# A linear-attention and GELU block: kv in 128-row blocks, 1/den by Ln and Exp, other places for the GpSimd adds of z

## The chip, the cores and the metric

One core of one Trainium2 chip. The metric is the device time of one execution in microseconds (us). TensorE does the matmuls, VectorE, ScalarE and GpSimd the elementwise work. In profile lines PE is TensorE, PEld its weight loads, DVE VectorE, ACT ScalarE, POOL GpSimd; L206 is line 206 of that kernel's file. Most executions of a kernel lie within 0.5 us, with a tail about 1 to 2 us higher; the trace comes from one execution.

## The reference, cut to what matters

```python
# x: (1, 2048, 640) bf16; H = 32 heads of 20 columns; F = 1536
xn  = layernorm(x)
q, k, v = split(xn @ wqkv)
pq, pk  = phi(q), phi(k)             # phi(t) = (t+1 if t > 0 else exp(t)) + 1e-6
kv  = einsum("bhsd,bhse->bhde", pk, v)
z   = einsum("bhsd->bhd", pk)        # sum of pk over the 2048 tokens
num = einsum("bhqd,bhde->bhqe", pq, kv)
den = einsum("bhqd,bhd->bhq", pq, z)[..., None] + 1e-6
out = x + (num / den) @ wo + gelu(xn @ w1 + b1) @ w2 + b2
```

## The kernel before

The 2048 tokens are 16 tiles of 128, in four groups of four. For each group g, TensorE makes K (tokens by columns), then Q (columns by tokens), then, for groups 0 to 2, twelve blocks of h = x1·w1, whose GELU ScalarE computes. While TensorE does h, VectorE makes the statistics, the reciprocal standard deviations (by Newton steps on 128x4 numbers) and the norms of the *next* group; TensorE transposes those tiles between the last h blocks. phi costs ScalarE an Exp and VectorE two operations for each 512 columns. The sum z of pk over tokens is gathered by GpSimd, one 128x640 add for each tile.

```python
def emit_norm(t, c0=0, c1=NC):                       # VectorE, bf16 in and out
    nc.vector.tensor_scalar(out=xn[:, t, ds], in0=x_all[:, t, ds],
        scalar1=mv[:, t, 0:1], scalar2=rstd[:, t : t + 1], op0=subtract, op1=mult)

def phi(dst, ps, shaped):
    nc.scalar.activation(out=e[:], in_=ps[:], func=ACT.Exp)
    nc.vector.tensor_scalar(out=e[:], in0=e[:], scalar1=1.0, scalar2=1e-6, op0=min, op1=add)
    nc.vector.scalar_tensor_tensor(out=dst, in0=shaped(ps), scalar=0.0, in1=shaped(e), op0=max, op1=add)

def emit_Kphi(t):
    ...
        if g > 0: emit_zacc(g)                       # adds of z behind the phi of K

def emit_zacc(g):                                    # 4 adds for a group, 3 for group 0
    for u in range(max(1, g * TPG), (g + 1) * TPG):
        nc.gpsimd.tensor_tensor(out=zsum if u == NT - 1 else zacc[:],
            in0=pk[:, 0, :] if u == 1 else zacc[:], in1=pk[:, u, :], op=ALU.add)

for g in range(NG):
    ...                                              # K and Q of group g
    for j in range(NJ if g < NG - 1 else 0):         # NJ = 12, TPG = 4
        emit_h(g, j)
        if g == 0 and j == NJ - 1:                   # hold GpSimd back to the last GELU
            nc.gpsimd.tensor_copy(out=Z3t[:, 0, 0:1], in_=hT[0][:, j, 0:1])
            emit_zacc(0)
            emit_masks()
        if j < TPG: emit_stats(t1 + j)
        if j == TPG: emit_rstd_vector(t1, t1 + TPG)  # Newton
        if TPG <= j < 2 * TPG: emit_norm(t1 + j - TPG)
        if j > 2 * TPG: emit_T(t1 + j - 2 * TPG - 1, nc.scalar.copy)
        if j == NJ - 1: emit_T(t1 + TPG - 1, nc.scalar.copy)
```

After the groups come G = xnᵀ·pk, den and its quotient (a VectorE reciprocal), then kv = wvᵀ·G for each window of heads and KVW = kv·wo, and last the output, in which `hT·w2` and `pqT·KVW` are added up in one bank.

```python
nc.vector.reciprocal(out=recT[:], in_=den[:])
...
for c in range(NC):                                  # kv: 25 matmuls of 140 columns
    for j in range(NC):
        nc.tensor.matmul(ps[:, 0:n], lhsT=wv[:, j, c*P:(c+1)*P], rhs=GT[:, j, h0*DH : h1*DH], ...)
    nc.vector.tensor_tensor(... gmask ...)
for m in range(NC):                                  # KVW: 26 matmuls of 320 columns, as the
    ...                                              # windows overlap the 128-row blocks
        for ic, c in enumerate(cs):
            nc.tensor.matmul(ps[:, 0:HALF], lhsT=kvT[:, c, m*P:(m+1)*P], rhs=wo[:, c, ns], ...)
```

## Time and profile before

| | before |
|---|---|
| median of 6 runs (range) | 217.94 us (217.52 to 218.53) |
| span of the profiled run, TensorE clock | 215.8 us, 1.0 |
| TensorE busy | 208.4 us |
| TensorE waits before the transposes of groups 1 and 2 | 1.42 and 0.31 us |
| kv, KVW (from their first matmul to the next matmul of h) | 1.57 and 3.53 us |

The busy line of the page of before, and the line of the chain of work that ended last, by engine. In the first, busy us, share of the span and instructions.

```profile
PE 208.4 (97%) x1373; PEld 120.8 (56%) x1390; DVE 108.2 (50%) x251; ACT 82.4 (38%) x132; POOL 55.3 (26%) x60
...
PE 74%; DVE 17%; ACT 3%; DMA 2%; issue 2%; SPq 0%; DVEq 0%
```

TensorE is at 97%, so the kernel gains only by fewer streamed columns or by fewer TensorE waits. The chain credits VectorE with 17%, but only because it follows VectorE's queue back from a wait; most of that time TensorE was busy as well. So read the waits themselves: below, TensorE's waits in before, with the releaser, us in total, number and longest.

```profile
PE mm L215 <- DVE xn L206: 2.0, 3, 1.4
PE mm L159 <- DVE hT_80 L128: 1.3, 1, 1.3
PE mm L236 <- ACT xnT L216: 0.5, 1, 0.5
```

L215 is the transpose, L206 the norm. Two of its three waits are in the loop. Now the timeline of before around the transposes of group 0 (start, us, engine, line, operation, in the last column the tensor written and those read, the count, and in brackets the idle time ahead of it).

```profile
29.07 1.51 DVE L206 TENSOR_SCALAR xn<-x_all,mv,rstd 128x640 bf16<-128x640 bf16 x4
...
29.72 0.44 PE L215 MATMUL mm<-identity,xn 128*128 128x128 bf16 x5
...
33.53 1.39 POOL L270 TENSOR_TENSOR zacc<-pk 128x640 f32<-128x640 bf16 x1
```

In group 0 the four norms run in 1.51 us, end at 30.58, and the transposes begin at 29.72 without a wait. GpSimd's adds come 3 us later. The same view of before, around group 1:

```profile
47.96 5.83 POOL L270 TENSOR_TENSOR zacc<-zacc,pk 128x640 f32<-128x640 f32 x4
...
52.37 0.17 DVE L188 TENSOR_SCALAR newton<-newton 128x4 int32<-128x4 int32 x1
52.57 1.25 DVE L192 TENSOR_SCALAR rstd<-newton 128x4 int32<-128x4 int32 x1
...
55.70 1.51 DVE L206 TENSOR_SCALAR xn<-x_all,mv,rstd 128x640 bf16<-128x640 bf16 x4
...
56.20 0.45 PE L215 MATMUL mm<-identity,xn 128*128 128x128 bf16 x5 [1.42 <-DVE xn L206]
```

Here GpSimd's four adds (5.83 us, so 1.46 each) lie beside VectorE's Newton steps. One of these takes 1.25 us where its neighbour takes 0.17: it stands until an add is over, at 53.8. The norms come late, and TensorE waits 1.42 us at 56.20. The last view of before is the timeline of the later stages:

```profile
105.91 3.36 DVE L402 RECIPROCAL recT<-mm 128x512 bf16<-128x512 f32 x1 [5.18 <-PE mm L397]
...
110.25 0.40 PE L409 MATMUL mm<-recT,Em_96 32*128 32x512 bf16 x4
...
124.46 1.73 PE L435 MATMUL mm<-GT,wv 128*128 128x140 bf16 x25
...
126.03 3.40 PE L288 MATMUL mm<-xnT,w_88 128*128 128x512 bf16 x14
...
129.26 3.69 PE L453 MATMUL mm<-wo,late 128*128 128x320 bf16 x26
...
132.79 1.24 PE L288 MATMUL mm<-xnT,w_88 128*128 128x512 bf16 x5
```

The reciprocal, on VectorE, ends at 109.27; its reader (L409) stands in TensorE's order behind other work and starts at 110.25 without a wait. kv runs from 124.46 to 126.03 and KVW from 129.26 to 132.79.

### The profile page before, as it was taken

How to read it: one execution, taken by the hardware profiler on the slowest of the kernel's cores; microseconds unless marked ns; L12 is line 12 of the kernel's file. 1: busy time of each engine (PE TensorE's matmuls, PEld its weight loads, DVE VectorE, ACT ScalarE, POOL GpSimd, SP SyncE). 2: the span in 40 equal slices, each digit the busy share in tenths (PEclk: the TensorE clock that was granted, in tenths of full speed). 3: DMA queues.
4: the chain of work that ended last, by engine and by line, in shares of the span. 5: the costliest groups of instructions: out<-in, count | busy, mean ns of one | idle time of the engine just before them, and what ended most of it. 6: DMA issues, size and time to landing. Idle time of an engine off the chain costs nothing.

```text
span 215.8 us, 3378 instructions
## 1 busy us (share of the span) xinstructions
PE 208.4 (97%) x1373; PEld 120.8 (56%) x1390; DVE 108.2 (50%) x251; ACT 82.4 (38%) x132; POOL 55.3 (26%) x60
## 2 busy tenths in 40 slices
PE   7899999999799999999999999999999999999994
PEld 2454455444454445545554565477777777777763
DVE  3878952999539992695374425812212212212211
ACT  3576779586686868751112746500000000000000
POOL 1000007899004600069999800000000000000000
PEclk9999999999999999999999999999999999999999
DMA  6999950000000000000000000000000010010011
GB/s 204 381 354 351 363 205 3 2 0 0 0 3 0 0 0 3 0 2 2 3 0 0 3 0 0 3 27 34 33 30 30 30 63 31 30 33 30 30 64 30
DMA packets 9727, 12.83 MB, mean 59 GB/s; under 512 B 2160, under 2 KB 8560, under 8 KB 9712
## 3 DMA queue, kind: packets, MB, share of 16 engines
q1 hardware_dynamic: 9712, 12.62, 17.1%
q8 instruction: 11, 0.18, 0.3%
q14 instruction: 4, 0.03, 0.1%
HBM read 10.00 MB, written 2.62 MB: 58 GB/s over the span
## 4 chain that ended last, share of the span: by engine, by line
PE 74%; DVE 17%; ACT 3%; DMA 2%; issue 2%; SPq 0%; DVEq 0%
PE mm L471 24%; PE mm L288 14%; PE mm L475 10%; PE mm L361 8%; PE mm L279 5%; PE mm L236 4%; DVE e L221 4%; DVE pk L224 3%; DVE pqT L224 3%; DVE stats L170 3%; PE mm L370 2%; DMA x_all<-in_A_x_dram 2%; PE mm L215 2%; PE mm L453 2%; ACT xnT L216 1%
## 5 line engine op out<-in xcount | busy, mean ns | idle before, releaser
L288 PE MATMUL mm<-xnT,w_88 128*128 128x512 bf16 x232 | 53.7, 379 | 0.4
L479 DVE TENSOR_TENSOR late<-mm,x_all 128x320 bf16<-128x320 f32 (+2 forms) x32 | 15.7, 491 | 58.5 <-PE mm L475 58.5
L288 PEld LDWEIGHTS <-w_88 128*128 128x128 bf16 x240 | 23.0, 98 | 26.2 <-issue 0.5
L220 ACT ACTIVATE e<-mm 128x512 bf16<-128x512 f32 x40 | 23.1, 597 | 12.9 <-PE mm L279 3.4
L221 DVE TENSOR_SCALAR e<-e 128x512 bf16<-128x512 bf16 x40 | 17.9, 448 | 19.2 <-ACT e L220 19.2
L270 POOL TENSOR_TENSOR zacc<-zacc,pk 128x640 f32<-128x640 f32 x13 | 18.3, 1408 | 34.5 <-DVE pk L224 33.6
L475 PE MATMUL mm<-late,pqT 128*128 128x320 bf16 (+2 forms) x160 | 27.0, 299 | 0.0
L279 PE MATMUL mm<-xnT,wqk 128*128 128x512 bf16 x98 | 22.0, 379 | 0.1
L353 POOL TENSOR_TENSOR x_all<-x_all,b2b 128x640 bf16<-128x640 bf16 x16 | 21.8, 1400 | 0.0
L236 PE MATMUL mm<-wqk,xnT 128*128 128x512 bf16 x77 | 19.9, 379 | 0.7 <-ACT xnT L216 0.5
L475 PEld LDWEIGHTS <-pqT 128*128 128x128 bf16 x160 | 15.5, 98 | 6.3
L361 PE MATMUL mm<-pk,xn 128*128 128x512 bf16 x77 | 17.8, 379 | 0.3 <-issue 0.2
L279 PEld LDWEIGHTS <-wqk 128*128 128x128 bf16 x100 | 9.6, 98 | 10.8
L414 DVE TENSOR_TENSOR pqT<-pqT,mm 128x512 bf16<-128x512 bf16 x20 | 12.3, 681 | 6.0 <-PE mm L409 6.0
L170 DVE BATCH_NORM_STATS2 stats<-x_all 128x6 f32<-128x320 bf16 x32 | 13.8, 467 | 2.7 <-DMA x_all<-in_A_x_dram 2.7
L471 PE MATMUL mm<-w_90,hT_82 128*128 128x320 bf16 x96 | 14.3, 299 | 0.0
L471 PE MATMUL mm<-w_90,hT_80 128*128 128x320 bf16 x96 | 14.3, 299 | 0.0
L471 PE MATMUL mm<-w_90,hT_81 128*128 128x320 bf16 x96 | 14.3, 299 | 0.0
L471 PE MATMUL mm<-w_90,hT_1148 128*128 128x320 bf16 (+2 forms) x95 | 14.3, 298 | 0.1
L224 DVE SCALAR_TENSOR_TENSOR pk<-mm,e 128x512 bf16<-128x512 f32 x20 | 13.8, 692 | 1.0
L224 DVE SCALAR_TENSOR_TENSOR pqT<-mm,e 128x512 bf16<-128x512 f32 x20 | 13.8, 692 | 0.7
L361 PEld LDWEIGHTS <-xn 128*128 128x128 bf16 x80 | 7.5, 98 | 9.1 <-issue 0.7
(70 smaller groups left out, 201.2 us busy)
## 6 DMA issues: line engine op xcount, KB each, us to landing
out_dram<-late SPq DMA_DIRECT2D x15, 160.0 KB, 1.8
x_all<-in_A_x_dram SPq DMA_DIRECT2D x3, 640.0 KB, 9.1
w_88<-in_B_w_dram SPq DMA_DIRECT2D x1, 1920.0 KB, 13.2
w_90<-in_B_w_dram SPq DMA_DIRECT2D x1, 1920.0 KB, 14.9
wqk<-in_A_wqkv_dram SPq DMA_DIRECT2D x1, 800.0 KB, 7.2
wv<-in_A_wqkv_dram SPq DMA_DIRECT2D x1, 800.0 KB, 8.6
wo<-in_A_wo_dram SPq DMA_DIRECT2D x1, 800.0 KB, 10.4
x_all<-in_A_x_dram SPq DMA_DIRECT2D x1, 480.0 KB, 3.8
```

The costliest lines, as they stand in the source:

```text
L170: nc.vector.bn_stats(out=st[:, half, :], in_=x_all[:, t, half * HALF : (half + 1) * HALF])
L220: nc.scalar.activation(out=e[:], in_=ps[:], func=ACT.Exp)
L221: nc.vector.tensor_scalar(out=e[:], in0=e[:], scalar1=1.0, scalar2=1e-6, op0=ALU.min, op1=ALU.add)
L224: nc.vector.scalar_tensor_tensor(out=dst, in0=shaped(ps), scalar=0.0, in1=shaped(e), op0=ALU.max, op1=ALU.add)
L236: nc.tensor.matmul(K_ps[t][:], lhsT=xnT[:, k, t * P : (t + 1) * P], rhs=wqk[:, k, D : D + TOK], start=(k == 0), stop=(k == NC - 1),)
L270: nc.gpsimd.tensor_tensor(out=zsum if u == NT - 1 else zacc[:], in0=pk[:, 0, :] if u == 1 else zacc[:], in1=pk[:, u, :], op=ALU.add,)
L279: nc.tensor.matmul(ps[:], lhsT=wqk[:, k, m * P : (m + 1) * P], rhs=xnT[:, k, gs], start=(k == 0), stop=(k == NC - 1),)
L288: nc.tensor.matmul(ps[:], lhsT=w1[:, k, j * P : (j + 1) * P], rhs=xnT[:, k, g * TOK : (g + 1) * TOK], start=(k == 0), stop=(k == NC - 1),)
L353: nc.gpsimd.tensor_tensor(out=x_all[:, t, :], in0=x_all[:, t, :], in1=b2b[:], op=ALU.add)
L361: nc.tensor.matmul(ps[:], lhsT=w, rhs=pk[:, t, 0:TOK], start=(t == 0), stop=(t == NT - 1))
L471: nc.tensor.matmul(ps, lhsT=hT[g][:, j, i * P : (i + 1) * P], rhs=w2[:, j, ns], start=(j == 0), stop=False)
L475: nc.tensor.matmul(ps, lhsT=pqT[:, c, t * P : (t + 1) * P], rhs=KVW[:, c, ns], start=False, stop=(c == NC - 1),)
```

## The change

Four parts, with these intents. (1) The start: x of tile 1 by itself, wk in other pieces, two transposes ahead of the first K, so that K runs without holes. (2) The adds of z move from behind phi to behind the norms, so that they do not run beside phi's VectorE work. (3) kv is formed in blocks of 128 of its rows that begin at head borders. What sticks out over 128 rows (12 or 32 rows) is packed on 32-row quadrants of TensorE, so kv has 25 full matmuls of 128 columns and 25 small ones, and KVW 10 of 128 rows and 10 of a quadrant instead of 26 full ones. (4) 1/den as exp(-ln(den + 1e-6)) on ScalarE.

```diff
-    load_x(1, 4)
-    load_wk(0, 2)
-    load_wk(2, NC)
+    load_x(1, 2)
+    load_wk(0, 3)
+    load_x(2, 4)
+    load_wk(3, NC)
...
-            if g > 0:
+            if g == NG - 1:
                 emit_zacc(g)
...
     emit_stats(0)
     emit_rstd(0, 1)
-    emit_stats_half(1, 0)
+    emit_stats(1)
+    emit_rstd(1, 2)
     emit_norm(0)
     emit_T(0, nc.scalar.copy, 0, 3)
-    emit_stats_half(1, 1)
-    emit_rstd(1, 2)
     emit_T(0, nc.scalar.copy, 3, NC)
+    emit_norm(1)
     emit_stats(2)
     emit_rstd(2, 3)
-    emit_norm(1)
-    emit_Ka(0, 0, 4)
     emit_T(1, nc.scalar.copy)
...   (K of tiles 0 to 2 in pieces around the transposes of tiles 2 and 3)
-            if g == 0 and j == NJ - 1:
-                nc.gpsimd.tensor_copy(out=Z3t[:, 0, 0:1], in_=hT[0][:, j, 0:1])
-                emit_zacc(0)
-                emit_masks()
+            if j == 2 * TPG:
+                nc.gpsimd.tensor_copy(out=Z3t[:, 0, 0:1], in_=hT[g][:, j - 1, 0:1])
+                emit_zacc(g)
+                if g == 0:
+                    emit_masks()
...
-        nc.vector.reciprocal(out=recT[:], in_=den[:])
+    nc.scalar.activation(out=lnden, in_=den[:], func=ACT.Ln, bias=tiny_t[:], scale=1.0)
+    nc.scalar.activation(out=recT[:], in_=lnden, func=ACT.Exp, scale=-1.0)
...   (kv: 128 rows from e_lo[m], the head border at or below 128*m)
+                kvps[a][:, i * P : (i + 1) * P], lhsT=wv[:, j, e_lo[m] : e_lo[m] + P],
+                rhs=GT[:, j, m * P : (m + 1) * P], start=(j == 0), stop=(j == NC - 1),
...   (the rests, each on 32 partitions)
+                    kvps[1][i * H : i * H + r, (a + 1) * P : (a + 2) * P],
+                    lhsT=wv[:, j, e_lo[m] + P : e_lo[m] + P + r],
+                    rhs=GT[:, j, m * P : (m + 1) * P], start=(j == 0), stop=(j == NC - 1),
...   (KVW, groups of four banks)
+            nc.tensor.matmul(ps[:, 0:HALF], lhsT=kv[:, m, :], rhs=woA[:, m, ns], start=True, stop=False)
...
+                ps[:, 0:HALF], lhsT=kv[q, NC + a, :], rhs=woB[q, a, ns], start=False, stop=True
...   (cut: masks for the new blocks, loads of wo in blocks, six output buffers instead of four)
```

The copy into `Z3t` exists only to hold GpSimd back. In the program it stands behind the norms of the group, but what it *waits for* is the eighth GELU of h, which knows nothing of VectorE.

More of the change, by code (lines that the diff above doesn't have):

```diff
@@ L49 @@
     assert REST * TPG == TOK and NG * H == P
-    win = []
-    for c in range(NC):
-        h_lo = (c * P) // DH
-        h_hi = (c * P + P - 1) // DH
-        win.append((h_lo, h_hi + 1))
+    e_lo = [m * P // DH * DH for m in range(NC)]
+    e_rest = [min(H, (m * P + P - 1) // DH + 1) * DH - e_lo[m] - P for m in range(NC)]
+    SKEW = DH - 4
+    assert all(0 < r <= H for r in e_rest) and all(m * P - e_lo[m] <= SKEW for m in range(NC))
     ctx.enter_context(nc.allow_non_contiguous_dma(reason="small strided setup transfers"))
@@ L80 @@
     w1 = consts.tile([P, NC, F], BF16, name="w1")
-    wo = consts.tile([P, NC, D], BF16, name="wo")
+    woA = consts.tile([P, NC, D], BF16, name="woA")
     w2 = consts.tile([P, NJ, D], BF16, name="w2")
@@ L92 @@
     eps_t = consts.tile([P, 1], F32, name="eps_t")
+    tiny_t = consts.tile([P, 1], F32, name="tiny_t")
     recT = consts.tile([P, TOK], BF16, name="recT")
@@ L124 @@
     nc.sync.dma_start(out=wv[:], in_=wqkv_v[:, :, 2 * D : 3 * D])
-    nc.sync.dma_start(out=wo[:], in_=A_wo.rearrange("(c p) n -> p c n", p=P))
+    for m in range(NC):
+        nc.sync.dma_start(out=woA[:, m, :], in_=A_wo[e_lo[m] : e_lo[m] + P, :])
     nc.sync.dma_start(out=w2[:], in_=w2_v)
@@ L129 @@
     nc.vector.memset(eps_t[:], EPS)
+    nc.vector.memset(tiny_t[:], 1e-6)
     make_identity(nc, identity)
@@ L154, in emit_masks, with emit_emask, select @@
             )
+    WIDE = SKEW + P + H
+    emask = zacc[:].bitcast(BF16)[:, 0 : (NC + 2) * WIDE].rearrange("p (b u) -> p b u", u=WIDE)
+    emask_u = emask[:, :, SKEW : SKEW + P]
+    def emit_emask():
+        def select(block, q, first, shift):
+            for base, sign in ((first, 1), (DH - 1 - first, -1)):
+                nc.gpsimd.affine_select(
+                    out=emask[q, block, SKEW - shift : SKEW - shift + H // 4 * DH],
+                    in_=emask[q, block, SKEW - shift : SKEW - shift + H // 4 * DH],
+                    compare_op=ALU.is_ge, fill=0.0, base=base,
+                    pattern=[[-sign * DH, H // 4], [0, DH]], channel_multiplier=sign,
+                )
+        nc.gpsimd.memset(emask, 1.0)
+        for m in range(NC):
+            select(m, slice(0, P), 0, m * P - e_lo[m])
+        for m in range(NC):
+            block, i = NC + m // NG, m % NG
+            select(block, slice(i * H, (i + 1) * H), P, m * P - e_lo[m])
     def emit_warm(n):
@@ L299 @@
     emit_rstd(0, 1)
-    emit_stats_half(1, 0)
+    emit_stats(1)
+    emit_rstd(1, 2)
     emit_norm(0)
     emit_T(0, nc.scalar.copy, 0, 3)
-    emit_stats_half(1, 1)
-    emit_rstd(1, 2)
     emit_T(0, nc.scalar.copy, 3, NC)
+    emit_norm(1)
     emit_stats(2)
     emit_rstd(2, 3)
-    emit_norm(1)
-    emit_Ka(0, 0, 4)
     emit_T(1, nc.scalar.copy)
-    emit_Ka(0, 4, NC)
-    emit_Kb(0)
     emit_stats_half(3, 0)
@@ L316 @@
     emit_rstd(3, 4)
-    emit_T(2, nc.vector.tensor_copy)
-    emit_Ka(1)
+    emit_norm(3)
+    emit_Ka(0)
+    emit_Kb(0)
+    emit_Ka(1, 0, 2)
+    emit_T(2, nc.scalar.copy)
+    emit_Ka(1, 2, NC)
     emit_Kb(1)
-    emit_norm(3)
+    emit_Kphi(0)
+    emit_Ka(2, 0, 1)
     emit_T(3, nc.scalar.copy)
-    emit_Kphi(0)
+    emit_Ka(2, 1, NC)
+    emit_Kb(2)
     emit_Kphi(1)
-    emit_K(2)
+    emit_Kphi(2)
     emit_K(3)
@@ L350 @@
                 emit_T(t1 + TPG - 1, nc.scalar.copy)
+    emit_emask()
     for t in range(NT):
@@ L400 @@
             )
-    with nc.allow_low_precision(reason="the quotient is used in bf16"):
-        nc.vector.reciprocal(out=recT[:], in_=den[:])
+    lnden = hT[NG - 1][:, NJ - 2 : NJ, :].rearrange("p a n -> p (a n)").bitcast(F32)
+    nc.scalar.activation(out=lnden, in_=den[:], func=ACT.Ln, bias=tiny_t[:], scale=1.0)
+    nc.scalar.activation(out=recT[:], in_=lnden, func=ACT.Exp, scale=-1.0)
     emit_G(2)
@@ L424 @@
     late = mid.tile([P, NT, D], BF16, name="late", tag="mid")
-    kvT = late[:, 0:NC, :]
-    KVW = late[:, NC : 2 * NC, :]
-    nc.gpsimd.memset(kvT, 0.0)
+    kv = late[:, 0:2, :].rearrange("p a n -> p (a n)")[:, 0 : (NC + 2) * P].rearrange("p (b n) -> p b n", n=P)
+    KVW = late[:, 2 : 2 + NC, :]
+    osbs = [late[:, 2 + NC + i, :] for i in range(6)]
+    woB = late[:, NT - 2 : NT, :]
+    for m in range(NC):
+        a, i = divmod(m, NG)
+        r = e_rest[m]
+        nc.sync.dma_start(
+            out=woB[i * H : i * H + r, a, :], in_=A_wo[e_lo[m] + P : e_lo[m] + P + r, :]
+        )
@@ L428 @@
     for j in range(4):
         emit_h(NG - 1, j)
-    for c in range(NC):
-        h0, h1 = win[c]
-        n = (h1 - h0) * DH
-        ps = bank()
+    kvps = [bank(), bank()]
+    for m in range(NC):
+        a, i = divmod(m, NG)
         for j in range(NC):
             nc.tensor.matmul(
-                ps[:, 0:n], lhsT=wv[:, j, c * P : (c + 1) * P], rhs=GT[:, j, h0 * DH : h1 * DH],
-                start=(j == 0), stop=(j == NC - 1),
-            )
-        nc.vector.tensor_tensor(
-            out=kvT[:, c, h0 * DH : h1 * DH].rearrange("p (h e) -> p h e", e=DH),
-            in0=ps[:, 0:n].rearrange("p (h e) -> p h e", e=DH),
-            in1=gmask[:, c, h0:h1].unsqueeze(2).to_broadcast((P, h1 - h0, DH)),
-            op=ALU.mult,
-        )
+                kvps[a][:, i * P : (i + 1) * P], lhsT=wv[:, j, e_lo[m] : e_lo[m] + P],
+                rhs=GT[:, j, m * P : (m + 1) * P], start=(j == 0), stop=(j == NC - 1),
+            )
@@ new lines @@
+    for a in range(2):
+        ms = range(a * NG, min(NC, (a + 1) * NG))
+        for j in range(NC):
+            for m in ms:
+                i = m % NG
+                r = min(H, D - e_lo[m] - P)
+                nc.tensor.matmul(
+                    kvps[1][i * H : i * H + r, (a + 1) * P : (a + 2) * P],
+                    lhsT=wv[:, j, e_lo[m] + P : e_lo[m] + P + r],
+                    rhs=GT[:, j, m * P : (m + 1) * P], start=(j == 0), stop=(j == NC - 1),
+                )
+    ps0 = kvps[0][:].rearrange("p (b n) -> p b n", n=P)
@@ L445 @@
+    ps1 = kvps[1][:].rearrange("p (b n) -> p b n", n=P)
+    nc.vector.tensor_tensor(out=kv[:, 0:NG, :], in0=ps0, in1=emask_u[:, 0:NG, :], op=ALU.mult)
+    nc.vector.tensor_tensor(
+        out=kv[:, NG : NG + 2, :], in0=ps1[:, 0:2, :], in1=emask_u[:, NG : NG + 2, :], op=ALU.mult
+    )
+    r = e_rest[NC - 1]
+    nc.vector.tensor_tensor(
+        out=kv[0:r, NG + 2, :], in0=ps1[0:r, 2, :], in1=emask_u[0:r, NG + 2, :], op=ALU.mult
+    )
     for j in range(4, 7):
         emit_h(NG - 1, j)
-    for m in range(NC):
-        cs = [c for c in range(NC) if win[c][0] * DH < (m + 1) * P and win[c][1] * DH > m * P]
-        for half in range(2):
+    for group in ([(m, 0) for m in range(NG)], [(m, 1) for m in range(NG)], [(NC - 1, 0), (NC - 1, 1)]):
+        pss = [bank() for _ in group]
+        for ps, (m, half) in zip(pss, group):
@@ L450 @@
             ns = slice(half * HALF, (half + 1) * HALF)
-            ps = bank()
-            for ic, c in enumerate(cs):
-                nc.tensor.matmul(
-                    ps[:, 0:HALF], lhsT=kvT[:, c, m * P : (m + 1) * P], rhs=wo[:, c, ns],
-                    start=(ic == 0), stop=(ic == len(cs) - 1),
-                )
-            if half == 0:
-                nc.scalar.copy(out=KVW[:, m, ns], in_=ps[:, 0:HALF])
-            else:
-                nc.vector.tensor_copy(out=KVW[:, m, ns], in_=ps[:, 0:HALF])
+            nc.tensor.matmul(ps[:, 0:HALF], lhsT=kv[:, m, :], rhs=woA[:, m, ns], start=True, stop=False)
@@ new lines @@
+        for ps, (m, half) in zip(pss, group):
+            ns = slice(half * HALF, (half + 1) * HALF)
+            a, i = divmod(m, NG)
+            q = slice(i * H, i * H + e_rest[m])
+            nc.tensor.matmul(
+                ps[:, 0:HALF], lhsT=kv[q, NC + a, :], rhs=woB[q, a, ns], start=False, stop=True
+            )
+        for n, (ps, (m, half)) in enumerate(zip(pss, group)):
+            ns = slice(half * HALF, (half + 1) * HALF)
+            (nc.vector.tensor_copy if n % 2 else nc.scalar.copy)(out=KVW[:, m, ns], in_=ps[:, 0:HALF])
@@ L481 @@
     for t in range(NT):
-        osb = late[:, 2 * NC + t % 4, :]
+        osb = osbs[t % len(osbs)]
         if t < NT - 1:
```

## The prediction

> **Bound now.** TensorE. The page gives PE 208.4 us of 215.8 (97%), clock 1.0 in all slices. The timeline shows its waits: 1.3 + 0.3 + 0.5 us before the first K matmul, 1.42 us before the first transpose of group 1 (54.78 to 56.20, on the VectorE norm) and 0.31 us before that of group 2 (81.26 to 81.57). The rest runs at the streaming rate: a 128x512 matmul takes 0.216 us of the chain, a 320-column one 0.136. Only fewer columns, or those waits, can pay.
>
> **Start.** Smaller first loads and K matmuls put behind two transposes: K should end about 0.2 us earlier (now 13.70), because ScalarE copies the second transpose only after rstd of tile 2. But VectorE then waits for b1 (DMA to 17.78), which does not move, so its norms for group 1 stay at 29.07 to 30.58 and the transposes at about 29.7. Worth 0 to 0.2 us.
>
> **z adds.** In before, the minimum-and-add of phi takes 0.28 us alone and 0.83 to 0.96 beside GpSimd adds or selects; one Newton step takes 1.25 instead of 0.17. The Trainium skill (SBUF — State Buffer, Who interferes with whom) has VectorE's two-port modes and two-SBUF-input ops blocked for a whole GpSimd instruction; the trace agrees: one such VectorE op per 1.46 us add. Moving z(1), z(2) away from phi and masks 5 us earlier frees about 2 to 3 us of VectorE in each of groups 1 and 2, so both norm waits vanish: -1.4 and -0.3 us.
> But the adds wait for the eighth GELU, not for the norms. In group 0 that GELU ends at 28.45, while VectorE is in its Newton steps until 29.07 and norms until 30.58. There the three adds will block the last Newton steps and norms: first norm done about 30.2 to 31.5 instead of 29.5, transposes at 29.7 wait. I expect a new TensorE wait of 1.4 us (0.7 to 2.5). In groups 1 and 2 the norms are about done when adds start; at most the last one is caught, harmlessly.
>
> **kv and KVW.** Before: 25 matmuls of 140 columns, 1.56 us; 26 of 320, 3.53 us. After: 25 of 128 columns, 1.4 us, plus 25 quadrant ones; from the den stage (20 in 1.19 us, then 0.16 of issue) 0.8 to 1.4 us. KVW: 10 x 0.136 = 1.36, plus 10 row-quadrant matmuls in three groups; from the four recT ones (0.33 plus 0.11 of changeover) 0.36 + 0.36 + 0.45. The skill (TensorEngine Tiling, Key Properties) says that changing mode drains TensorE; those 0.11 to 0.16 us agree. Sum 4.8 to 5.3 against 5.1: nothing, +-0.3.
>
> **1/den.** Reciprocal 3.36 us on VectorE becomes two ScalarE passes of 0.6. It ended at 109.27, needed at 110.25: off the path, 0. Mask and output-buffer changes: 0; GpSimd's residual adds end near 126, needed at 141.
>
> **Sum:** 217.9 - 0.1 + 1.4 - 1.4 - 0.3 - 0.05 = 217.5 us; range 215.9 to 219.1. Faster by over 2%: 0.03; within: 0.96; slower: 0.01.
>
> **Right or wrong shows in:** the timeline around 28 to 35 us (norms stretched from 0.38 to over 1 us, a transpose wait); no wait at groups 1 and 2; phi's min-add near 0.3 us there; kv and KVW stretch of about 5 us; ScalarE Ln and Exp without a table load between.
>
> **What would make it wrong:** norms escaping the adds in group 0 (then about 216.1); Newton steps blocked one per add (219); quadrant matmuls much cheaper or dearer than den suggests; a start gain that reaches VectorE; a table load for Ln.

## The result, and the profile after

| | before | after |
|---|---|---|
| median (range, runs) | 217.91 us (217.42 to 220.5, 40) | 217.33 us (216.86 to 219.48, 20) |
| ratio of fast runs, 95% interval | | 0.9973 (0.995 to 0.9995) |

A ratio here is the mean time of one kernel's fast runs over the mean of the other's of the same rounds, so it is not quite the ratio of the medians quoted. None of the 20 runs of after was slow (their clocks are 0.998 to 1.0), and the outputs are correct. The gain is 0.3%, within the 2% that counts as the same.

The runs of after come in two heaps: counting the profiled one, 14 of 21 took 216.9 to 217.6 us and 7 took 218.3 to 219.9. The trace of after is one of the upper heap (219.9 us, a span of 218.0), so it looks worse than before, which the median is not. Before has an upper heap too: 9 of its 40 runs took 219.0 to 220.5 us. None of those was traced, so a heap by itself does not show what made it. The busy line of after and its chain line:

```profile
PE 208.8 (96%) x1392; PEld 120.2 (55%) x1409; DVE 106.9 (49%) x248; ACT 84.3 (39%) x135; POOL 60.9 (28%) x82
...
PE 71%; DVE 17%; DMA 6%; SPq 2%; ACT 2%; issue 1%; DVEq 0%
```

Its waits of TensorE (L239 is the transpose, L260 the K matmul):

```profile
PE mm L239 <- DVE xn L230: 2.5, 2, 1.9
PE mm L183 <- DVE hT_80 L130: 1.3, 1, 1.3
PE mm L260 <- DMA wqk<-in_A_wqkv_dram: 0.9, 1, 0.9
PE mm L260 <- ACT xnT L240: 0.6, 1, 0.6
```

The waits of groups 1 and 2 should have gone, yet the norms still hold TensorE for 2.5 us. The timeline of after shows where. Group 0:

```profile
30.16 1.39 POOL L294 TENSOR_TENSOR zacc<-pk 128x640 f32<-128x640 bf16 x1
30.18 1.39 DVE L224 SCALAR_TENSOR_TENSOR rstd<-newton,rstd 128x4 f32<-128x4 f32 x1
...
31.61 3.98 DVE L230 TENSOR_SCALAR xn<-x_all,mv,rstd 128x640 bf16<-128x640 bf16 x4
...
33.27 0.45 PE L239 MATMUL mm<-identity,xn 128*128 128x128 bf16 x5 [1.90 <-DVE xn L230]
```

The first add starts at 30.16, and the last Newton step, at 30.18, takes 1.39 us instead of 0.16. The four norms behind it take 3.98 us instead of 1.51. TensorE waits 1.90 us at 33.27; before had no wait there. Group 1 of after:

```profile
57.31 4.84 DVE L230 TENSOR_SCALAR xn<-x_all,mv,rstd 128x640 bf16<-128x640 bf16 x4
...
57.50 5.94 POOL L294 TENSOR_TENSOR zacc<-zacc,pk 128x640 f32<-128x640 f32 x4
...
62.21 0.45 PE L239 MATMUL mm<-identity,xn 128*128 128x128 bf16 x5 [0.55 <-DVE xn L230]
```

The adds start 0.19 us after the first norm. The norms take 4.84 us, but only the last transpose finds its norm missing (0.55 us); the 1.42 us wait of before is gone. In group 2 no transpose waits. The start of after:

```profile
7.99 0.89 DVE L194 BATCH_NORM_STATS2 stats<-x_all 128x6 f32<-128x320 bf16 x2 [1.64 <-DMA x_all<-in_A_x_dram]
8.89 0.59 PE L260 MATMUL mm<-wqk,xnT 128*128 128x512 bf16 x2 [0.89 <-DMA wqk<-in_A_wqkv_dram]
...
10.32 0.60 PE L260 MATMUL mm<-wqk,xnT 128*128 128x512 bf16 x2 [0.56 <-ACT xnT L240]
...
15.01 1.24 PE L303 MATMUL mm<-xnT,wqk 128*128 128x512 bf16 x5
```

The statistics of tile 2 wait 1.64 us for their x, K waits 0.89 us for wk and 0.56 us for ScalarE's copy of the second transpose. Q begins at 15.01; in before it began at 13.53. The late stages of after:

```profile
127.00 1.56 PE L470 MATMUL mm<-GT,wv 128*128 128x128 bf16 x25
128.48 0.73 PE L480 MATMUL mm<-GT,wv 128*32 128x128 bf16 x25
...
132.40 0.71 PE L501 MATMUL mm<-woA,late 128*128 128x320 bf16 x4
133.04 0.31 PE L506 MATMUL mm<-late 12*128 12x320 bf16 x4
```

kv's full matmuls take 1.48 us (127.00 to 128.48), its 25 quadrant ones 0.67 (h follows at 129.15). KVW takes 2.53 (h follows at 134.93).

To add this up without being misled by one execution, I read from several traces when the same matmuls start. us between these marks:

| stretch | before | after, first trace | after, second trace |
|---|---|---|---|
| start to first Q matmul | 13.53 | 15.01 | 14.47 |
| to first transpose of group 0 | 16.19 | 18.26 | 16.77 |
| to K of group 1 | 3.27 | 3.60 | 3.59 |
| to first transpose of group 1 | 23.21 | 21.62 | 21.62 |
| to K of group 2 | 3.28 | 4.00 | 3.28 |
| to first transpose of group 2 | 22.09 | 21.63 | 21.62 |
| to K of group 3, on to kv | 42.89 | 42.88 | 42.88 |
| kv, h between, KVW | 8.33 | 7.93 | 7.93 |
| rest | 83.0 | 83.1 | 83.0 |

The second trace (below) is of the lower heap, with a span of 215.2. Against before: start +0.94, group 0 +0.90, group 1 -1.59, group 2 -0.47, kv and KVW -0.40, in sum -0.6, which is the difference of the spans. The two traces of after differ by 2.8 us: 1.5 in group 0, 0.7 at the last transpose of group 1, and 0.5 at the start.

### The profile page after: what moved, and what is told of

Read it like the earlier page. It is cut to its first block, busy times and chain, and to the rows that moved or that the text cites. A ratio compares the mean times of both kernels' runs of the same rounds, so it can differ in the third digit from the quotient of the medians.

```text
span 218.0 us, 3463 instructions
## 1 busy us (share of the span) xinstructions
PE 208.8 (96%) x1392; PEld 120.2 (55%) x1409; DVE 106.9 (49%) x248; ACT 84.3 (39%) x135; POOL 60.9 (28%) x82
## 3 DMA queue, kind: packets, MB, share of 16 engines
HBM read 10.10 MB, written 2.62 MB: 58 GB/s over the span
## 4 chain that ended last, share of the span: by engine, by line
PE 71%; DVE 17%; DMA 6%; SPq 2%; ACT 2%; issue 1%; DVEq 0%
PE mm L522 24%; PE mm L312 12%; PE mm L526 10%; PE mm L389 8%; DMA b_bf<-in_B_b_dram 6%; PE mm L303 5%; PE mm L260 4%; DVE xn L230 4%; DVE pqT L248 3%; DVE stats L194 3%; PE mm L398 2%; DVE e L245 2%; DVE pk L248 2%; DVE rstd L224 1%; PE mm L270 1%
## 5 line engine op out<-in xcount | busy, mean ns | idle before, releaser
L245 DVE TENSOR_SCALAR e<-e 128x512 bf16<-128x512 bf16 x40 | 14.7, 367 | 16.9 <-ACT e L244 16.9
L260 PE MATMUL mm<-wqk,xnT 128*128 128x512 bf16 x77 | 19.9, 379 | 1.7 <-DMA wqk<-in_A_wqkv_dram 0.9
L230 DVE TENSOR_SCALAR xn<-x_all,mv,rstd 128x640 bf16<-128x640 bf16 x16 | 12.1, 800 | 1.2 <-ACT rstd L205 1.1
```

Of the source, the lines that this page charges most:

```text
L260: nc.tensor.matmul(K_ps[t][:], lhsT=xnT[:, k, t * P : (t + 1) * P], rhs=wqk[:, k, D : D + TOK], start=(k == 0), stop=(k == NC - 1),)
```

## The experiments

### The changed kernel again

No edit; a second trace and ratio.

> The changed kernel, untouched, for a second trace and a second ratio. My theory of the first trace of it: its start was held up by late loads in that one execution (the third x and wk pieces landed near 7.9 and 8.9 us, the b1 load 1.3 us later than before), which is scatter between executions. If so, this trace has the group 0 transposes at about 31 us instead of 33.3, still with a TensorE wait there of 1 to 2 us, and the ratio is near 0.997. Rival: the smaller, reordered loads are late in every execution; then the K stage again ends near 15 us (13.7 in before).

Measured: 217.12 us median (216.92 to 217.16, 5 runs) against 217.67, ratio 0.9974 (0.9962 to 0.9986). Its timeline around group 0:

```profile
29.60 1.39 POOL L294 TENSOR_TENSOR zacc<-pk 128x640 f32<-128x640 bf16 x1
29.62 4.86 DVE L230 TENSOR_SCALAR xn<-x_all,mv,rstd 128x640 bf16<-128x640 bf16 x4
...
31.24 0.45 PE L239 MATMUL mm<-identity,xn 128*128 128x128 bf16 x5 [0.41 <-DVE xn L230]
```

This time the add starts (29.60) just after the last Newton step and catches only the norms: they take 4.86 us, but one gets through in the gap before each next add, and the first transpose waits 0.41 us, not 1.90. So the wait between 1 and 2 us that I expected was too large for this execution. Q starts at 14.47. In the four traces of the whole new start it begins at 14.37 to 15.01, and in the eight of the old start at 13.40 to 13.97. So my theory of scatter explains about 0.5 us of the first trace, and the rival is right about the rest: the loss at the start is in every one of them, 0.94 us here, though smaller than its 15 us.

### Only what the adds wait for

```diff
-                nc.gpsimd.tensor_copy(out=Z3t[:, 0, 0:1], in_=hT[g][:, j - 1, 0:1])
+                nc.gpsimd.tensor_copy(out=Z3t[:, 0, 0:1], in_=xn[:, t1 + TPG - 1, 0:1])
```

> One edit to the changed kernel: the GpSimd copy that holds back the adds of z reads the last norm of the group instead of the eighth GELU. My theory (the adds hold up the last Newton step and the norms, and those the transposes): the four norms of group 0 take 1.5 us instead of 4.0, the TensorE wait before the first transpose of group 0 falls from 1.9 to under 0.4 us, the wait of 0.55 in group 1 goes too, and the kernel gains 1.3 to 2 us: ratio to before 0.989 to 0.993. Rival (the wait comes from VectorE being late because of the start and the b1 load): the norms begin late anyway, the wait stays above 1 us and the time is as that of the changed kernel, 0.997.

Measured: 216.13 us (215.93 to 216.37, 5 runs), ratio 0.993 (0.9918 to 0.9941), on the chip where the changed kernel took 217.12. The timeline around group 0:

```profile
29.61 1.52 DVE L230 TENSOR_SCALAR xn<-x_all,mv,rstd 128x640 bf16<-128x640 bf16 x4
...
30.55 0.44 PE L239 MATMUL mm<-identity,xn 128*128 128x128 bf16 x5
...
31.34 1.40 POOL L294 TENSOR_TENSOR zacc<-pk 128x640 f32<-128x640 bf16 x1
```

The norms are back to 1.52 us, no transpose of groups 0 to 2 waits, and the adds start behind the norms. The whole gain is 1.0 us, less than the 1.3 to 2 expected, since those came from the first trace and its upper heap. The rival, that VectorE is late for other reasons, is refuted: nothing but the adds moved, and the norms begin at the same time as in the second trace of after (29.61 against 29.62).

### Only the adds, on the kernel before

The two hunks of the diff that concern `emit_zacc`, nothing else.

> Only the move of the adds of z, on the kernel before. My theory: a new wait of 1 to 2 us at the transposes of group 0, the waits of 1.42 and 0.31 us in groups 1 and 2 gone or below 0.6 together; net between -0.8 and +0.5 us, ratio 0.996 to 1.002. Rival (moving the adds is a clean gain, and it is the start that costs the time): a gain of 1.5 us or more, ratio 0.993 or less.

Measured: 218.69 us median, in a wide spread: 216.78 (the profiled run), and 218.34 to 219.73 in the five timed ones; ratio 1.0041 (1.0009 to 1.0072). In its trace the last Newton step runs from 28.77 to 28.94 and the first add starts at 28.88, so the step was under way and was not held. TensorE waits 0.41 us in group 0 and not at all in groups 1 and 2. For that execution it is a net gain of 0.9 us, as my theory has it in kind, but the wait is smaller than the 1 to 2 us that I gave. The five timed executions were slower than the range I gave. The adds alone are a gamble that mostly lost on this chip. What exactly the losing executions do, this trace cannot say.

### Only the start, on the kernel before

The loads and the order of the first K matmuls, nothing else.

> Only the new order of loads and of the first K matmuls, on the kernel before. My theory: K ends 0 to 0.3 us earlier, and nothing of it reaches the transposes of group 0, since VectorE waits for b1 at about 17.8 us: ratio 0.998 to 1.002. Rival: the small loads come late, K ends 1 us or more later (near 15 us) and the kernel loses about 1 us, ratio 1.004 to 1.006.

Measured: 218.39 us (218.13 to 218.44, 5 runs), ratio 1.0032 (1.0019 to 1.0045). My theory fell. The rival held in kind: the new start costs 0.7 us, less than the 1 us that it gave. The trace has Q at 14.41, with waits of 0.8 us for wk and 0.6 for the copy, as in after.

### Only kv and KVW, on the kernel before

> Only the new kv and KVW stage (with its masks, loads of wo and output buffers) and, as it needs them, nothing of the other parts, on the kernel before. From the trace of the changed kernel: kv 2.15 us instead of 1.56, KVW 2.53 instead of 3.53, sum 4.68 instead of 5.09, so a gain of 0.4 us: ratio 0.997 to 0.999. If the stage is worth more than its own stretch (shorter evacuations, a GpSimd memset less), the gain is 1 us or more, ratio 0.995 or less.

Measured: 217.31 us (217.16 to 217.42, 6 runs) against 217.70, ratio 0.9963 (0.9931 to 0.9995; three runs of before were near 219.2, which pulls the ratio down). By medians the gain is 0.39 us. In its trace kv takes 2.16 us and KVW 2.54, together 4.70 against 5.10 in before. The stage is worth its own stretch.

### Only 1/den, on the kernel before

> Only the quotient by Ln and Exp on ScalarE, on the kernel before. Both theories of the whole: VectorE's 3.36 us go, two ScalarE passes of about 0.6 us come, no table load between, and TensorE waits for neither: ratio 0.999 to 1.001. If the quotient was on the path after all, the gain is over 0.5 us, ratio under 0.998.

Measured: 217.77 us (4 runs) against 217.70, ratio 0.9999 (0.9953 to 1.0046): unclear by its interval, no gain by the medians. The timeline of this run:

```profile
105.87 0.69 ACT L404 ACTIVATE hT<-mm,tiny_t 128x512 f32<-128x512 f32 x1 [1.51 <-PE mm L399]
...
106.59 0.63 ACT L405 ACTIVATE recT<-hT 128x512 bf16<-128x512 f32 x1
```

0.69 and 0.63 us in place of 3.36, with no table load between, as the nearest loads in its ScalarE timeline are at 86.34 and 120.59. TensorE reads the quotient at 110.20, as before.

### Old start, adds that wait for the norms

The changed kernel with both corrections.

```diff
-    load_x(1, 2)          # and the rest of the new start
+    load_x(1, 4)          # and the rest of the old start
...
-                nc.gpsimd.tensor_copy(out=Z3t[:, 0, 0:1], in_=hT[g][:, j - 1, 0:1])
+                nc.gpsimd.tensor_copy(out=Z3t[:, 0, 0:1], in_=xn[:, t1 + TPG - 1, 0:1])
```

> The changed kernel with the loads and the first K matmuls in the old order, and with the GpSimd copy reading the last norm of the group. My theory is that the parts add up: start 0 instead of +0.7 us, no transposes waiting in groups 0 to 2 (-1.7), kv and KVW -0.4: 2.1 us under before, ratio 0.989 to 0.992, faster than the changed kernel and than the one with only the late adds. Rival: the new start pays elsewhere, by letting VectorE run ahead, and taking it back gains nothing: ratio 0.993 as with the late adds alone.

Measured: 215.28 us (215.08 to 215.44, 6 runs) against 217.70, ratio 0.9868 (0.9834 to 0.9903, helped by the same three runs of before; the medians give 0.9889). The parts add up to more than the 2.1 us expected: 2.4. This version beats both kernels (the changed kernel took 217.12 and 217.33 us, but in other rounds). The chain line of its page:

```profile
PE 95%; DMA 2%; issue 1%; DVE 0%; ACT 0%; SPq 0%
```

The 17% of VectorE in the chain is gone: from the first K on, TensorE never waits for it.

### The adds alone, a second look

> The kernel before with only the adds moved, for a second trace: its first was profiled in its fastest execution (216.8 us), the five timed ones took 218.3 to 219.7. My theory of the spread: it depends on which VectorE operation the first add of group 0 catches. If it catches a Newton step as well as the first norm, the first transpose waits 1.4 us longer (1.9 instead of 0.4) and the run takes about 218.5; if it comes just after the last Newton step, the wait is 0.4 and the run takes about 217. A trace of either kind has to fit this. Rival: the slow executions are slow elsewhere (start, loads), with the same wait of 0.4.

Measured: 216.42 us, one run, so its state is unknown. The first add starts at 28.52, 0.01 us after the last Newton step; the wait is 0.41 us. It fits the lower half of the theory, but it was the fast kind again, and so it gives no view of the slow one.

### New loads alone, and new order alone

> Only the new cut of the loads at the start, first K matmuls in the old order, on the kernel before. Theory A (the loads cost it: the last piece of wk now lands at 8.2 us, after a fifth descriptor and behind the x of tiles 2 and 3, where its slices were in use at 7.5 in before): TensorE waits 0.5 to 1 us for wk, K ends near 14.3 us instead of 13.7, ratio 1.002 to 1.004. Theory B (the order costs it: ScalarE copies the second transpose only behind rstd of tile 2): K ends at 13.7, ratio 0.999 to 1.001.

> Only the new order of the first K matmuls, with the old loads, on the kernel before. Theory A (the loads cost it): at most 0.3 us later, ratio up to 1.0015. Theory B (the order costs it): the second K block waits for its transpose's copy by 0.6 us or more, and K ends at 14.2 or later, ratio 1.002 to 1.004. In this mix the statistics of tile 1 also stand ahead of the first norm while its x still comes with tiles 2 and 3, which can add up to 0.6 us to either.

Measured: the loads alone 218.37 us against 218.00, ratio 1.0004 (0.9968 to 1.004); the order alone 218.70, ratio 1.0022 (0.9981 to 1.0062). Both are unclear. The profile of the loads alone fell in a throttled execution (clock 0.661, span 315.1), so its times are not used. What was waited for at the start can still be read from it, as the clock was 1.0 for the first 6 us and the statistics took their usual 0.89 us for two: those of tile 2 wait 1.39 us for their x, until 7.21, and K waits 0.38 us for wk. With the order alone they start at 7.02 without a wait, and K does not wait for wk. So both waits come with the new cut of the loads. In the trace of the order alone Q starts at 14.95, but its first five K matmuls took 2.1 us instead of 1.1 for a reason that the trace does not show, and their wait for the copy is not there. So neither A nor B is shown as the cause of the lost time. It stays open how the 0.7 us divide between the loads and the order.

### Holding back group 0 only

On the kernel before with the adds moved:

```diff
-                nc.gpsimd.tensor_copy(out=Z3t[:, 0, 0:1], in_=hT[g][:, j - 1, 0:1])
+                nc.gpsimd.tensor_copy(out=Z3t[:, 0, 0:1],
+                    in_=(xn[:, t1 + TPG - 1, 0:1] if g == 0 else hT[g][:, j - 1, 0:1]))
```

> On the kernel before, the adds of z moved, those of group 0 held back by the group's last norm, those of groups 1 and 2 by the eighth GELU as in the change. My theory: the wait of group 0 goes and with it the spread, the gain of groups 1 and 2 stays (1.4 + 0.3): 1.4 to 1.8 us under before, ratio 0.992 to 0.994, runs within 0.5 us of each other. Rival (groups 1 and 2 are a gamble too): a spread of over 1 us stays.

Measured: 217.90 us (217.50 to 218.18, 6 runs) against 218.00, ratio 0.9981 (0.9948 to 1.0014). Not the 1.4 to 1.8 us gain; the timeline around group 1 says why:

```profile
53.90 5.83 POOL L270 TENSOR_TENSOR zacc<-zacc,pk 128x640 f32<-128x640 f32 x4
54.01 5.90 DVE L206 TENSOR_SCALAR xn<-x_all,mv,rstd 128x640 bf16<-128x640 bf16 x4
...
55.54 0.45 PE L215 MATMUL mm<-identity,xn 128*128 128x128 bf16 x5 [0.48 <-DVE xn L206]
...
59.97 0.45 PE L215 MATMUL mm<-identity,xn 128*128 128x128 bf16 x5 [1.02 <-DVE xn L206]
```

Group 0 is clean now (its first transpose at 30.00, no wait). But in group 1 the adds start at 53.90, the norms at 54.01, and now the norms of group 1 lose: 5.90 us for the four, with waits of 0.48 and 1.02 us. So group 1 is a gamble as well, as the rival had it, though not with the spread that it gave: these six runs lie within 0.7 us.

Why group 1 lost here and not in the first trace of the adds alone, the two traces narrow down. Counted from the first K matmul of group 1, the adds start at nearly the same place (20.63 us behind it here, 20.76 there), but the first norm starts at 20.74 instead of 19.95. Half of this shift is that phi begins 0.39 us later behind that matmul. The other half is that its ten minimum-and-adds take 4.21 us instead of 3.80, while GpSimd, held back in group 0, ends its masks at 11.3 instead of 8.6. That the delayed masks cause this half is argued; no run tests it.

### The adds one GELU earlier in group 0

Worse on purpose (correct results):

```diff
-    in_=hT[g][:, j - 1, 0:1])
+    in_=hT[g][:, j - (2 if g == 0 else 1), 0:1])
```

> Wrong on purpose: as the adds alone, but those of group 0 start one GELU (1.08 us) earlier, well inside the Newton steps. My theory of the spread (an add that catches a Newton step costs one add length more before the first norm): in every run the first transpose waits 1.9 us or more, and the time is 218.3 us or more, as in the slow executions of the adds alone, with no fast ones left. Rival (the spread has another cause): a mix of 216.5 and 219 as before, with a wait near 0.4.

Measured: 219.08 us median of 4 (218.40, 218.41 at full clock; 219.74 and 221.77 at a clock of 0.992). The last counts as slow; the ratio of the other three is 1.0027 (0.9975 to 1.0079), not clear of the noise. The profiled run is the one of 219.74. Its timeline around group 0, and the clock line of its page (40 slices of 5.45 us):

```profile
27.65 1.41 POOL L270 TENSOR_TENSOR zacc<-pk 128x640 f32<-128x640 bf16 x1
27.83 1.25 DVE L199 TENSOR_TENSOR newton<-newton,rstd 128x4 f32<-128x4 f32 x1
...
30.79 1.25 DVE L200 SCALAR_TENSOR_TENSOR rstd<-newton,rstd 128x4 f32<-128x4 f32 x1
...
32.57 0.71 PE L215 MATMUL mm<-identity,xn 128*128 128x128 bf16 x5 [2.62 <-DVE xn L206]
...
33.08 2.34 PE L288 MATMUL mm<-xnT,w 128*128 128x512 bf16 x5
...
PEclk9999997999999999999999999999999999999999
```

Each of the three adds holds one Newton step for 1.25 us (the second at 29.31), the norms behind them are free again, and TensorE waits 2.62 us. All four executions took over 218.3 us, as expected. That adds which catch Newton steps cost TensorE more than adds which catch only norms is shown: 2.62 us for three steps here, 1.90 for one and the norms behind it in the first trace of after, 0.41 for norms alone.

This wait also cost more than its length. Behind it the granted clock of TensorE fell to 0.5 (0.54, 0.50, 0.50 and 0.76 in the four us from 32 on), and five matmuls of h took 2.34 us instead of 1.24. From the first transpose to K of group 1 it took 4.70 us, 1.43 more than in before. That is about what this execution took beyond the two at full clock (1.3 us). Behind the 1.90 us wait in the first trace of after the clock stayed at 1.0.

That the upper heap of after consists of executions that caught a Newton step is shown for one of them, its first trace, and argued for the others. The upper heap of before, where no adds lie beside the norms of group 0, shows that there may be another cause, which no run tested.

## Why the prediction was right or wrong

The time was right: 217.5 predicted, 217.33 measured, in the range and within 2%. It was right in part by luck, because the misses nearly cancelled: in the second trace of after the start came out 1.0 us worse than its term, group 0 0.5 us better, groups 1 and 2 and the kv stage 0.4 us better each.

- **Bound now: right.** TensorE, and only its columns and waits count. The version without the two loop waits and with the new kv stage (0.4 us) is 2.4 us faster.
- **Start, "Worth 0 to 0.2 us": wrong**, and the largest miss. It cost: +0.7 us alone, +0.94 in the second trace of after. I had foreseen that ScalarE copies the second transpose only behind rstd of tile 2, but took the x of tiles 2 and 3, and wk, to arrive in time. That x now stands behind 480 KB of wk: in before the statistics of tile 2 started at 6.47 without a wait, in the first trace of after at 7.99 after one. And K needed wk before its last piece was there (0.8 to 0.9 us).
- **z in groups 1 and 2, "-1.4 and -0.3 us": right in mechanism**; the stretches shortened by 1.59 and 0.47, as less of the adds lies beside phi and the Newton steps (phi's ten minimum-and-adds take 3.97 and 2.84 us in the second trace, 4.95 and 5.06 in before). But the norms were not "about done when adds start": in group 1 the adds start 0.19 and 0.45 us after the first norm began. I called it harmless that the last norm might be caught there; the first trace (0.55 us) and the run that held back group 0 alone (1.5 us of waits) show that it isn't.
- **z in group 0, "a new TensorE wait of 1.4 us (0.7 to 2.5)": right in mechanism.** The term measured +0.90 in the second trace and +2.40 in the first (16.19 to 18.26 and 3.27 to 3.60). Removing the collision gained 1.0 us. The rule that I used is the Trainium skill's (SBUF — State Buffer, Who interferes with whom): VectorE's two-port modes contend with GpSimd, and its operations with two SBUF inputs with a GpSimd instruction that reads SBUF; the one that starts first blocks the other for the whole instruction. These traces agree: 0.16 becomes 1.39 us for a Newton step with two SBUF inputs, while the statistics (one SBUF input) take 0.83 us for two beside the adds and apart from them.
- **kv and KVW, "Sum 4.8 to 5.3 against 5.1": the mechanism right, one term mis-sized.** 4.68 measured, a gain of 0.40. KVW came out at the estimate (2.53). The quadrant matmuls of kv took 0.67 us, not 0.8 to 1.4, since I scaled them from the den stage, whose matmuls stream 512 columns. The Trainium skill (TensorEngine Tiling (Array Packing), Instruction Overhead) gives an overhead of about 60 cycles for each matmul; with the 2.4 GHz that the page Trainium Kernel Development and Optimization gives under NeuronCore Architecture this makes an estimate of 25 x 25 ns = 0.63 us. It comes near, but by luck: the trace's start times are not 27 ns apart. The first 20 matmuls start in five rounds of four, each round within 11 ns and 55 to 67 ns behind the one before; the last five, all on one quadrant, start one by one, 55 to 56 ns apart. So a round of four quadrants costs about as much as one full matmul of 128 columns (1.48 us for 25, 59 ns each), and so does a quadrant alone.
- **1/den, "off the path, 0": right.**

The sum with the measured terms of the second trace is +0.94 + 0.90 - 2.06 - 0.40 = -0.62 us; the medians differ by 0.58.

## What to carry to other kernels

Program order on one engine does not put work behind another engine's: make the held-back instruction wait for the very result that it must not disturb (here a copy that reads the last norm, not a GELU that usually ends about then). Where one engine blocks another for a whole instruction, a fraction of a us in timing decides over 1.5 us, so take more than one trace before you size the term, and expect that curing one collision can shift the next stage into one. Test the parts of a bundled change singly: here one part's loss hid another's gain.

## What the Trainium skill lacked or had wrong

- SBUF — State Buffer, Who interferes with whom: the rule held, but the page does not say what back-to-back GpSimd instructions leave open. Here about one VectorE operation got through at each border of two adds: the four norms, 1.51 us alone, took 4.86 beside adds 1.46 us apart, and GpSimd lost nearly no time.
- TensorEngine Tiling (Array Packing): it gives no price for changing the tiling mode. Four quadrant matmuls of 320 columns between full ones took 0.24 us in all (133.04 to 133.28), changeovers included; one full matmul of that width takes 0.136.
- ScalarE: Activation LUTs, Table sets: that ln and exp share a set is confirmed (0.69 and 0.63 us, no load between). Nothing lacking there.
- No page that I used sizes what cutting and reordering the first loads costs the loads behind them: x of tiles 2 and 3 held up its reader until 7.99 us (first trace of after) instead of 6.47. With the new loads alone that reader also waited for it, 1.39 us until 7.21; with the new order of matmuls alone it did not.
